# Ranking a planner's steps by the latest time they may begin, in an attention and two-layer kernel on one core

## The chip, the core and the metric

The kernel runs on one core of a Trainium2 chip. The metric is the device time of one execution in microseconds (us), smaller being better. A profile of one execution is at hand beside three timed runs.

The core has engines that run side by side, each with its own queue of instructions: TensorE (PE) multiplies matrices, and PEld is its loading of weights; VectorE (DVE) and ScalarE (ACT) do elementwise work and read the results from TensorE's accumulation banks; GpSimd (POOL) does a little elementwise work; SyncE (SP) here only issues DMAs. An instruction that waits for another engine holds up what stands behind it in its own queue.

## The reference

For 4 batches, 12 heads, 448 positions and 64 columns a head, in float32:

```python
scores = q @ k.T / sqrt(64) - log(448)
x = sigmoid(scores) @ v              # laid out as 1792 tokens x 768
h = x @ w_in                         # 768 x 2048
x = (h * cos(h)) @ w_out             # 2048 x 768
g, val = x @ w_gate, x @ w_val       # 768 x 1536 each
out = (g * sigmoid(g) * val) @ w_out2  # 1536 x 768
```

## The kernel before

**Numbers in two parts.** A float32 operand is split into a high part that TensorE takes at full speed (a copy to that type, mostly on ACT) and a low part (the operand minus the high part, always on DVE). A product is then three matmuls: high x high, high x low, low x high. The first needs only the high parts, so TensorE can begin a product whose low part is still missing, and then stops after one or two matmuls.

**Attention** (lines 511 to 625) comes first, in an order written out by hand. Its result X1 is kept as high and low parts in two large tiles, x0 and x1, one for each half of the tokens.

**The first layer** is 8 chunks of 256 columns of w_in by 4 groups of 448 tokens. For each such unit TensorE does two *ups* (18 matmuls each, line 863), then h*cos(h) is made of each result (`h_cos_h`, line 639, and `split_g`), and three *downs* of 12 matmuls (line 720) multiply it by w_out. DVE adds each pair of down results into R (`accumulate`, line 674), which frees the two banks for a later down.

**The second layer** has its tokens in two halves h of 896, and 6 chunks each, so 12 units. A unit multiplies by w_gate (u = 0) and by w_val (u = 1), each as a 2x2 block product in seven products, numbered 1 to 7, where sums of blocks of X and of the weights stand in for the eighth (`seven`, line 741). They run in the order 1, 5, 2, 6, 7, 3, 4 with downs of the unit before them in between (`TWO`). The seven X operands of a half are made from R by `inputs` (line 480), a step per operand: for 5, 6, 7 and 4 a difference of blocks (DVE), then the high part (`to_hi`, line 488: ACT or DVE, whichever the planner expects to end first), then the low part (DVE). Operands 1, 5, 2, 6 lie in x0 and 7, 3, 4 in x1, over the operands that were there: those of the first layer, later those of the half before. The rest of x1 lends room to weight operands.

Weights arrive by DMA in tiles `t`; `operands` (line 383) splits them in pairs (products 1 and 2; 6 and 3; 7 and 4) and singly (5), and makes the sums of weight blocks in four steps (`combine`, line 386) on DVE or POOL. The line 236 is the helper through which nearly all DVE sums and differences go, 233 that of most ACT instructions, so a tile's name tells more than its line.

**Conversions** (line 299). Of weights that come in 64 bits a word the kernel makes float32 tiles first: a load to `raw`, six steps on ACT and DVE (lines 309 to 324, the last a sum on `cv` that the rows call ISA or CUSTOM), a store to scratch memory, from where `loads` fetches them as `t`. They go on from the attention until the end of the first half of the second layer. When they end, `raw` is lent to `loads` and to others.

**What sets the order.** Nothing of this is ordered by hand after the attention: all steps are tasks of a small planner (class `Order`). Its `run` repeats one choice. Of all tasks whose inputs it reckons to be there it takes the one with the least

```python
key = (start, task.rank)
```

where `start` is the reckoned time at which engine and input are both free. So the rank decides among steps that are ready when an engine comes free. Before, a rank goes by the kind of task and is given at `spawn`: 0 for TensorE's own sequence and the copies between its banks, 1 and 2 for other banks' work (`accumulate` 2), 2.5 to 3 for the activations and `h_cos_h` with its `split_g`, 3 for loads, 3.5 for `inputs`, 4 for weight operands, 6 for conversions. The planner only writes the instructions down in this order, engine by engine; on the chip each engine runs its list in order and waits on semaphores.

Of the kernel before, what the change touches and what calls it, by code (L numbers as in the profile page):

```python
# [73 lines left out]
class Order:  # L74
# [4 lines left out]

    def __init__(self):  # L80
        self.busy, self.ready, self.open, self.now = {}, [], 0, 0.0
# [14 lines left out]
    def advance(self, task, sent=None):  # L96
        now = self.now
        while True:
# [51 lines left out]
def block_kernel(  # L150
# [104 lines left out]


# [22 lines left out]
    for need in needs():  # L279
        for w, f, i, _ in need:  # L280
            if w.dtype == U64 and (w, f + i) not in todo:
                todo.append((w, f + i))
    todo = iter(todo)
# [15 lines left out]
    def conversions(raw=None, t=None, back=None):  # L299

        while not (back and ended):
# [3 lines left out]
            if not back:  # L305
                raw = yield raws
            yield move(raw.rearrange("p n two -> p (n two)"), flat(w[f]).bitcast(I32))
            yield LANDING
            yield act(0.95, out=raw[:, :, 0], in_=raw[:, :, 0].bitcast(U32), func=AF.Copy, scale=2.0 ** -29)
# [3 lines left out]
            yield absolute(t, raw[:, :, 1])  # L313
            yield {"DVE": 0.6}, lambda _: nc.vector.tensor_scalar(
                t, t, HI_MOST, HI_LEAST, op0=ALU.min, op1=ALU.max
            )
            yield {"DVE": 0.6}, lambda _: nc.vector.tensor_scalar(
                ti, ti, 3, 0x3FFFFFF8, op0=ALU.logical_shift_left, op1=ALU.bitwise_and
            )
# [3 lines left out]
            )  # L323
            yield vec(1.0, ti, ti, raw[:, :, 0], ADD)
# [58 lines left out]
    def operands():  # L383


        def combine(out, a, b, op):
# [3 lines left out]
            return {"DVE": 0.6, "POOL": 1.3}, do  # L390
# [9 lines left out]
        def lower(keys, s, t, lo, hi, size, room, free, done):  # L400
            yield vec(0.1 + size / 780, lo, t, f32(hi), SUB)
# [9 lines left out]
        def split(keys, t, free=None):  # L411
# [4 lines left out]
            yield copy(0.15 + size / 980, hi, t)  # L416
# [21 lines left out]
        for n in range(n_first, n_units):  # L438
            for u in range(2):
# [6 lines left out]
                yield combine(sums, a21, a22, ADD)  # L446
                yield combine(a21, a11, a21, SUB)
# [32 lines left out]
    def inputs(h):  # L480
# [158 lines left out]
    def h_cos_h(key, h, read):  # L639
# [3 lines left out]
        yield act(0.55, out=u, in_=h, func=AF.Copy, scale=INV2PI, bias=0.25)  # L643
        yield act(0.6, out=f, in_=u, func=AF.Copy, bias=MAGIC)
        yield {"DVE": 0.65}, lambda _: nc.vector.scalar_tensor_tensor(  # L645
            out=f, in0=f, scalar=MAGIC, in1=u, op0=ALU.subtract, op1=ALU.subtract
        )
        yield act(0.6, out=u, in_=f, func=AF.Sin, scale=-TWO_PI)
        yield vec(0.65, f, u, h, ALU.mult)
# [3 lines left out]
    def silu(z, h, read, done):  # L653
        yield act(0.6, out=z, in_=h, func=AF.Silu)
# [3 lines left out]
    def silu_val(key, z, z_done, h, read, free):  # L658
        yield z_done
        yield vec(0.65, z, z, h, ALU.mult)  # L660
# [13 lines left out]
    def accumulate(n, j, d, first):  # L674
# [3 lines left out]
        two, acc = banks[:, first:first + 2, :N], R[h][:, j, d:d + 2]  # L678
        if c == 0:
# [3 lines left out]
            yield copy(1.05, acc, two)  # L683
        else:
            yield vec(1.1, acc, two, acc, ADD)
# [50 lines left out]
    PRODUCT = 0.2025  # L736

    TWO = "15d26d73d4"
    LAST = ("1526d734", "15d26d73d4dd")

    def seven(n, u, turn, z, downs):
# [7 lines left out]
        def first_copy():  # L749
            got["b"] = yield b  # L750
            yield copy(0.55, got["b"], got["a"])
            copied.set()

        def second_copy():
            got["e"] = yield e
            yield copy(0.55, got["e"], got["a"])
            apart.set()

        def fifth():
            yield copy(0.55, keep["12"], got["d"])  # L760
            d.give(got["d"])

        def sum22():
            yield vec(0.65, keep["22"], keep["12"], got["a"], ADD)
# [3 lines left out]
        def sum12():  # L768
            yield vec(0.65, keep["12"], keep["12"], got["e"], ADD)
# [3 lines left out]
        def after(ij, h, read):  # L773
            key = (n, int(ij[0]) - 1, int(ij[1]) - 1)
            if not val:
# [4 lines left out]
                order.spawn(silu(z[ij][0], h, read, z[ij][1]), 2.5)  # L780
            else:
                if ij in ("22", "12"):
                    read = shared_keep
                order.spawn(silu_val(key, z[ij][0], z[ij][1], h, read, z[ij][2]), 3)

        for token in LAST[u] if n == n_units - 1 else TWO:
# [183 lines left out]
```

## Time and profile before

| | us |
|---|---|
| median of 3 timed runs | 1148.28 |
| lowest and highest of them | 1145.71, 1149.85 |
| profiled execution, its own time | 1157.76 |
| its span, first to last instruction | 1155.9 |
| PE busy in it | 1122.1 |
| DVE busy | 807.5 |
| ACT busy | 573.1 |
| POOL busy | 80.1 |

The profiled execution is 9.48 us above the median. The page's slices show PE full but for the attention at the start (the first four slices), two places, at about 620 to 680 us and at 870 to 900 us, and the end. The rows that matter stand below under their own heading.

### The profile page before, as it was taken

The page shows a single profiled execution, that of the slowest core. Times are in us where ns is not written, and L with a number is a line of the kernel's source. Part 1 is how long each engine was busy: PE and PEld are TensorE (multiplying, and loading weights), DVE is VectorE, ACT ScalarE, POOL GpSimd, SP SyncE. Part 2 cuts the span into 40 slices and gives each one's busy share as a digit, 9 for nine tenths or more (in the row PEclk, how much of TensorE's full clock was granted, in tenths as well). Part 3 has the DMA queues.
Part 4 walks back from the last instruction along what each step waited for, and adds up shares of the span by engine and source line. Part 5 has one row for each costly group of instructions (what it writes and reads, how often), then busy time and mean ns, then how long its engine had stood idle before and what let it go on. Part 6 is the DMA issues. An engine that isn't in the chain of part 4 may idle for free.

```text
span 1155.9 us, 14399 instructions
## 1 busy us (share of the span) xinstructions
PE 1122.1 (97%) x5531; PEld 964.1 (83%) x5531; DVE 807.5 (70%) x1143; ACT 573.1 (50%) x858; POOL 80.1 (7%) x69
## 2 busy tenths in 40 slices
PE   9999999999999999999999799999997999999998
PEld 4555569999999999999998589999996999999996
DVE  6777745677777777777768967787888555556654
ACT  6877765645454544444444556443434344333330
POOL 0000000000000000000001110112203011102100
PEclk9999999999999999999999799999998999999999
DMA  9999723524343434334341334524321421121102
GB/s 251 286 277 264 206 109 125 166 98 145 110 150 110 150 110 142 118 123 138 109 137 41 109 124 148 181 88 157 138 84 59 143 83 55 55 69 55 49 8 96
DMA packets 51909, 146.43 MB, mean 127 GB/s; under 512 B 5760, under 2 KB 21120, under 8 KB 51840
## 3 DMA queue, kind: packets, MB, share of 16 engines
q1 hardware_dynamic: 51696, 145.28, 39.6%
q8 instruction: 43, 0.70, 0.2%
q10 hardware_dynamic: 144, 0.23, 0.1%
q14 instruction: 26, 0.21, 0.1%
HBM read 113.25 MB, written 32.24 MB: 126 GB/s over the span
## 4 chain that ended last, share of the span: by engine, by line
PE 89%; DVE 5%; DMA 4%; ACT 1%; issue 1%; SPq 0%; ACTq 0%; DVEq 0%
PE banks L720 35%; PE banks L809 27%; PE banks L863 21%; DMA raw<-in_qk 3%; PE banks L583 3%; PE banks L559 2%; PE banks L586 1%; DVE x L236 1%; DVE r L236 1%; DMA vs<-in_v 1%; DMA r<-in_w_out 1%; PE banks L571 1%; ACT a L549 0%; DVE r L320 0%; DVE x L530 0%
## 5 line engine op out<-in xcount | busy, mean ns | idle before, releaser
L720 PE MATMUL banks<-g,wb 128*128 128x448 f32 x1080 | 244.5, 368 | 1.2 <-DVE g L236 1.1
L236 DVE TENSOR_TENSOR r<-banks,r 128x896 f32<-128x896 f32 x144 | 156.9, 1090 | 117.8 <-PE banks L720 116.6
L720 PEld LDWEIGHTS banks<-g,wb 128*128 128x128 f32 x1080 | 202.8, 188 | 21.3 <-DVE g L236 1.4
L720 PE MATMUL banks<-g,wa 128*128 128x448 f32 x792 | 181.6, 368 | 1.7 <-DVE g L236 1.4
L720 PEld LDWEIGHTS banks<-g,wa 128*128 128x128 f32 x792 | 148.5, 188 | 16.7 <-DVE g L236 1.8
L809 PE MATMUL banks<-x,wb 128*128 128x448 f32 x666 | 149.5, 373 | 8.2 <-DVE x L236 5.4
L809 PEld LDWEIGHTS banks<-x,wb 128*128 128x128 f32 x666 | 127.0, 191 | 21.3 <-DVE x L236 6.5
L863 PE MATMUL banks<-x,wb 128*128 128x448 f32 x648 | 139.7, 368 | 0.0
L863 PEld LDWEIGHTS banks<-x,wb 128*128 128x128 f32 x648 | 121.6, 188 | 12.3
L233 ACT ACTIVATE g<-u 128x448 fp32r<-128x448 f32 x106 | 61.2, 578 | 142.5 <-DVE u L236 130.3
L233 ACT ACTIVATE u<-banks 128x448 f32<-128x448 f32 x106 | 57.4, 541 | 134.6 <-PE banks L863 79.5
L233 ACT ACTIVATE u<-u 128x448 f32<-128x448 f32 x148 | 85.3, 576 | 65.6 <-DVE u L645 34.8
L863 PE MATMUL banks<-x,wa 128*128 128x448 f32 x504 | 108.5, 369 | 0.0
L236 DVE TENSOR_TENSOR u<-u,banks 128x448 f32<-128x448 f32 x126 | 77.4, 614 | 41.5 <-PE banks L809 34.2
L863 PEld LDWEIGHTS banks<-x,wa 128*128 128x128 f32 x504 | 94.6, 188 | 9.9 <-issue 0.4
L809 PE MATMUL banks<-x,wa 128*128 128x448 f32 x432 | 94.7, 366 | 0.7 <-ACT banks L233 0.7
L809 PEld LDWEIGHTS banks<-x,wa 128*128 128x128 f32 x432 | 81.0, 188 | 8.0 <-ACT banks L233 1.1
L809 PE MATMUL banks<-x,x 128*128 128x448 f32 x315 | 73.4, 382 | 8.7 <-DVE x L236 8.6
L236 DVE TENSOR_TENSOR g<-u,g 128x448 fp32r<-128x448 f32 x106 | 68.6, 650 | 15.0 <-ACT g L233 14.9
L645 DVE SCALAR_TENSOR_TENSOR u<-u 128x448 f32<-128x448 f32 x64 | 39.9, 624 | 52.0 <-ACT u L233 51.5
L809 PEld LDWEIGHTS banks<-x,x 128*128 128x128 f32 x315 | 61.9, 198 | 15.6 <-DVE x L236 9.0
L549 ACT ACTIVATE a<-banks,r 128x896 f32<-128x896 f32 x72 | 67.2, 1003 | 7.2 <-PE banks L559 7.1
(88 smaller groups left out, 1274.2 us busy)
## 6 DMA issues: line engine op xcount, KB each, us to landing
raw<-in_w_out SPq DMA_DIRECT2D x22, 768.0 KB, 4.6
raw<-in_qk SPq DMA_DIRECT2D x47, 224.0 KB, 8.6
raw<-in_w_gate SPq DMA_DIRECT2D x12, 768.0 KB, 4.5
raw<-in_w_val SPq DMA_DIRECT2D x12, 768.0 KB, 4.7
vs<-in_v SPq DMA_DIRECT2D x24, 320.0 KB, 6.9
t<-swv SPq DMA_DIRECT2D x20, 384.0 KB, 3.1
t<-swg SPq DMA_DIRECT2D x19, 384.0 KB, 3.9
t<-swd SPq DMA_DIRECT2D x34, 192.0 KB, 2.5
```

What stands on the lines that cost most here:

```text
L233: return {"ACT": time}, lambda _: nc.scalar.activation(**kw)
L236: return {"DVE": time}, lambda _: nc.vector.tensor_tensor(out=out, in0=in0, in1=in1, op=op)
L549: nc.scalar.activation(out=a, in_=sc, func=AF.Sigmoid, bias=nlog, scale=1.0 / math.sqrt(D))
L559: nc.tensor.matmul(sc[:, j], lhsT=k[half, m, c * P:(c + 1) * P], rhs=q[half, p], start=n == 0, stop=n == 2,)
L571: nc.tensor.matmul(sc, lhsT=kb[:, m], rhs=q[:, p], start=n == 0, stop=n == 2)
L583: nc.tensor.matmul(o[half], lhsT=vw[:, 2 * c + j], rhs=a[:, j], start=c == 0, stop=False)
L586: nc.tensor.matmul(o, lhsT=block[:, 1], rhs=prob.pop((i, NCH)), start=False, stop=True)
L645: yield {"DVE": 0.65}, lambda _: nc.vector.scalar_tensor_tensor(out=f, in0=f, scalar=MAGIC, in1=u, op0=ALU.subtract, op1=ALU.subtract)
L720: nc.tensor.matmul(banks[:, first + e - d, :N], lhsT=w[:, m, e % KH if layer == 2 else e, :], rhs=g[:, p], start=(i, m, p) == (0, 0, 0), s ...
L809: nc.tensor.matmul(bank, lhsT=w[:, m, k, :], rhs=x[:, k, p, :], start=(k, m, p) == (0, 0, 0) and i in (1, 5), stop=(k, m) == (KH - 1, 1), ...
L863: nc.tensor.matmul(out, lhsT=w[:, m, k, :], rhs=x[:, k, p, cols], start=(k, m, p) == (0, 0, 0), stop=(k, m) == (KD - 1, 1),)
```

## The change

Every step beside TensorE now gets a rank of its own: the latest time at which it may begin if TensorE is never to wait for it. A table `due` is made beforehand from TensorE's sequence alone: the start of each up, product and down when all matmuls follow each other without a gap at 0.2025 us. A step's rank is the start of what waits for it less an allowance for the steps that come in between. The planner takes the rank from the step (`advance`) and is otherwise as it was: `start` still comes first in the key. TensorE's own sequence is the same. A down's `accumulate` is ranked by the down after the next; an X operand's steps by the product in which it is first used; a conversion by the first use of its weights less 25 us. Tasks that only issue DMAs for loads keep rank 3.

```diff
@@ Order.advance
-                task.wants, task.do = want
+                task.wants, task.do, task.rank = want if len(want) > 2 else (*want, task.rank)
@@ block_kernel, after units
+    time = 0.0
+    for key, products in steps():
+        due[key] = time
+        time += products * PRODUCT
+    end = time
...
+    def by(time, step):
+        return (*step, time)
@@ conversions
+                uses.setdefault((id(w), 2 * c + i), due[key] - 25.0)
...
-            yield absolute(t, raw[:, :, 1])
+            yield by(time, absolute(t, raw[:, :, 1]))
@@ operands
-            yield vec(0.1 + size / 780, lo, t, f32(hi), SUB)
+            yield by(due[keys[0]] - 1.2, vec(0.1 + size / 780, lo, t, f32(hi), SUB))
...
-                yield combine(a11, sums, a11, SUB)
-                yield combine(a12, a12, a11, SUB)
+                yield combine(a11, sums, a11, SUB, due[n, u, 6] - 4.0)
+                yield combine(a12, a12, a11, SUB, due[n, u, 3] - 4.0)
@@ inputs
+            time = due[n_first + h * (NF2 // 2), 0, i]
             if parts:
-                yield vec(1.6, t, parts[0], parts[1], SUB)
+                yield by(time - 5.0, vec(1.6, t, parts[0], parts[1], SUB))
             hi, lo = X[i][:, :, 0], X[i][:, :, 1]
-            yield to_hi(hi, t)
-            yield vec(1.6, lo, t, f32(hi), SUB)
+            yield by(time - 3.2, to_hi(hi, t))
+            yield by(time - 1.7, vec(1.6, lo, t, f32(hi), SUB))
@@ split_g (the like in h_cos_h, silu, silu_val, and the copies and sums of seven)
+        time = due["down", n, j, 0]
-        yield copy(0.6, g[:, 0], f)
-        yield vec(0.65, g[:, 1], f, f32(g[:, 0]), SUB)
+        yield by(time - 1.5, copy(0.6, g[:, 0], f))
+        yield by(time - 0.8, vec(0.65, g[:, 1], f, f32(g[:, 0]), SUB))
@@ accumulate
+        time = after_down(n, j if layer == 2 else 0, d) - 1.3
+        if layer == 1 and c == NF1 // 2 - 1:
+            time = min(time, due[n_first + h * (NF2 // 2), 0, 1] - 6.0)
-            yield vec(1.1, acc, two, acc, ADD)
+            yield by(time, vec(1.1, acc, two, acc, ADD))
```

TensorE's instructions stand in the same order as before, and no engine's order differs within the attention. The rows below are those of DVE at two places. In them r0 and r1 are the two halves of R, x0 and x1 hold the X operands and, at their rest, weights; `x<-r` is a low part (or, as CAST, a high part) of an X operand, `r<-r` the difference of blocks before it, `r<-banks` an accumulate, `wb<-t`, `wa<-raw` and `x1<-raw0` low parts of weights, and `g` an operand of the downs.

DVE where the first layer ends and the second begins, before:

```order
L314 TENSOR_SCALAR cv_1480<-cv_1480 128x768
L236 TENSOR_TENSOR g2_1486<-u2_1490,g2_1486 128x448
L493 CAST x0_66<-r0_64 128x3x448
L645 SCALAR_TENSOR_TENSOR u0_1488<-u0_1488 128x448
L236 TENSOR_TENSOR r1_65<-banks_63,r1_65 128x896
L236 TENSOR_TENSOR u0_1488<-u0_1488,banks_63 128x448
L236 TENSOR_TENSOR x0_66<-r0_64,x0_66 128x3x448
L236 TENSOR_TENSOR r1_65<-banks_63,r1_65 128x896
L236 TENSOR_TENSOR g3_1487<-u0_1488,g3_1487 128x448
L236 TENSOR_TENSOR wb0_1481<-t_68,wb0_1481 128x768
L236 TENSOR_TENSOR x0_66<-r0_64,x0_66 128x3x448
L236 TENSOR_TENSOR x1_67<-sum_1479,x1_67 128x384
```

and now:

```order
L395 TENSOR_SCALAR cv_1480<-cv_1480 128x768
L237 TENSOR_TENSOR x0_66<-r0_64,x0_66 128x3x448
L237 TENSOR_TENSOR g2_1486<-u2_1490,g2_1486 128x448
L237 TENSOR_TENSOR r1_65<-banks_63,r1_65 128x896
L727 SCALAR_TENSOR_TENSOR u0_1488<-u0_1488 128x448
L237 TENSOR_TENSOR wb0_1481<-t_68,wb0_1481 128x768
L237 TENSOR_TENSOR u0_1488<-u0_1488,banks_63 128x448
L237 TENSOR_TENSOR r1_65<-banks_63,r1_65 128x896
L237 TENSOR_TENSOR g3_1487<-u0_1488,g3_1487 128x448
L237 TENSOR_TENSOR x1_67<-sum_1479,x1_67 128x384
L237 TENSOR_TENSOR x0_66<-r0_64,x0_66 128x3x448
L237 TENSOR_TENSOR wb1_1482<-t_68,wb1_1482 128x768
```

The CAST, a high part of operand 5, has left DVE's list, as has that of operand 4 further down: all seven high parts stand on ACT now. The low part of operand 5 and the weights wb0 stand earlier, and the first step on the last chain for the downs (line 645, now 727) stands behind an accumulate.

DVE where the first half of the second layer ends and the second half begins, before:

```order
L236 TENSOR_TENSOR r0_64<-banks_63,r0_64 128x896
L236 TENSOR_TENSOR u2_1490<-u2_1490,u1_1489 128x448
L236 TENSOR_TENSOR g3_1487<-u2_1490,g3_1487 128x448
L236 TENSOR_TENSOR u0_1488<-u0_1488,banks_63 128x448
L236 TENSOR_TENSOR g2_1486<-u2_1490,g2_1486 128x448
L236 TENSOR_TENSOR x0_66<-r1_65,x0_66 128x3x448
L236 TENSOR_TENSOR g1_1485<-u0_1488,g1_1485 128x448
L236 TENSOR_TENSOR r1_65<-r1_65 128x1344
L236 TENSOR_TENSOR wb2_1483<-t_68,wb2_1483 128x768
L236 TENSOR_TENSOR wa0_69<-raw0_1477,wa0_69 128x768
L236 TENSOR_TENSOR x1_67<-r1_65,x1_67 128x3x448
L236 TENSOR_TENSOR x1_67<-raw0_1477,x1_67 128x768
```

and now:

```order
L237 TENSOR_TENSOR wb2_1483<-t_68,wb2_1483 128x768
L237 TENSOR_TENSOR r1_65<-r1_65 128x1344
L237 TENSOR_TENSOR x1_67<-raw0_1477,x1_67 128x768
L237 TENSOR_TENSOR u0_1488<-u0_1488,banks_63 128x448
L237 TENSOR_TENSOR r0_64<-banks_63,r0_64 128x896
L237 TENSOR_TENSOR u2_1490<-u2_1490,banks_63 128x448
L237 TENSOR_TENSOR x1_67<-sum_1479,x1_67 128x384
L237 TENSOR_TENSOR x0_66<-r1_65,x0_66 128x3x448
L237 TENSOR_TENSOR g1_1485<-u2_1490,g1_1485 128x448
L237 TENSOR_TENSOR r1_65<-r1_65 128x1344
```

The weights of products 1 and 2 of the new half, `x1<-raw0`, stood last of these and stand third now, ahead of the accumulate, the low part of operand 6 and the difference for operand 7. Two of the values `g2` and `g3` have gone behind what is shown.

## Rows read from the trace of the kernel before

**Rows 1.** The page's head and its line of TensorE: busy us, share, instructions.

```profile
span 1155.9 us, 14399 instructions
PE 1122.1 (97%) x5531; PEld 964.1 (83%) x5531; DVE 807.5 (70%) x1143; ACT 573.1 (50%) x858; POOL 80.1 (7%) x69
```

**Rows 2.** Whom PE waited for: total us, times, longest.

```profile
PE banks L809 <- DVE x L236: 14.0, 4, 8.6
...
PE banks L720 <- DVE g L236: 2.5, 2, 1.4
PE banks L809 <- DVE x L493: 2.2, 1, 2.2
```

**Rows 3.** Stretches: us; PE, PEld, DVE, ACT, POOL busy; clock; DMA share; GB/s.

```profile
160.00:622.00 462.00, 462.00 (x2237) 419.56 (x2237) 336.01 (x462) 235.28 (x373) 2.04 (x2) 1.00 0.38 129
622.00:672.00 50.00, 39.62 (x166) 33.47 (x164) 44.35 (x45) 23.66 (x33) 9.79 (x6) 0.86 0.30 95
672.00:876.00 204.00, 203.83 (x1006) 188.89 (x1007) 156.18 (x207) 99.46 (x152) 33.34 (x29) 1.00 0.38 126
876.00:896.00 20.00, 11.37 (x43) 10.03 (x42) 17.07 (x18) 8.71 (x13) 6.32 (x3) 0.74 0.17 50
```

**Rows 4.** PE in order of time between the layers: start, us, instruction, idle before.

```profile
645.78 0.47 PE L809 MATMUL banks<-x,wb 128*128 128x448 f32 x1 [0.62 <-ACT banks L233]
646.82 2.10 PE L809 MATMUL banks<-x,wb 128*128 128x448 f32 x9 [0.57 <-DVE x L236]
652.12 3.36 PE L809 MATMUL banks<-x,wb 128*128 128x448 f32 x8 [3.20 <-DVE x L236]
657.65 0.74 PE L809 MATMUL banks<-x,wb 128*128 128x448 f32 x1 [2.17 <-DVE x L493]
659.98 3.36 PE L809 MATMUL banks<-x,wb 128*128 128x448 f32 x8 [1.59 <-DVE x L236]
```

**Rows 5.** DVE in order of time, same place.

```profile
623.67 1.54 DVE L493 CAST x<-r 128x1344 fp32r<-128x1344 f32 x1
...
648.02 1.77 DVE L236 CUSTOM_DVE_ANT_0 cv<-raw,cv 128x1536 uint16<-128x1536 uint16 x1
...
656.05 1.54 DVE L493 CAST x<-r 128x1344 fp32r<-128x1344 f32 x1
...
658.38 1.55 DVE L236 TENSOR_TENSOR x<-r,x 128x1344 fp32r<-128x1344 f32 x1
...
661.58 0.55 DVE L314 TENSOR_SCALAR cv<-cv 128x768 f32<-128x768 f32 x1
...
663.76 0.96 DVE L236 CUSTOM_DVE_ANT_0 cv<-raw,cv 128x1536 uint16<-128x1536 uint16 x1
```

**Rows 6.** PE in order of time between the halves of the second layer.

```profile
878.39 0.57 PE L809 MATMUL banks<-x,x 128*128 128x448 f32 x2
887.59 6.32 PE L809 MATMUL banks<-x,x 128*128 128x448 f32 x16 [8.63 <-DVE x L236]
```

**Rows 7.** DVE in order of time, same place.

```profile
856.70 1.09 DVE L236 TENSOR_TENSOR r<-banks,r 128x896 f32<-128x896 f32 x1
...
876.76 1.09 DVE L236 TENSOR_TENSOR r<-banks,r 128x896 f32<-128x896 f32 x1 [1.04 <-PE banks L720]
...
885.12 1.55 DVE L236 TENSOR_TENSOR x<-r,x 128x1344 fp32r<-128x1344 f32 x1
886.59 0.95 DVE L236 TENSOR_TENSOR x<-raw,x 128x768 fp32r<-128x768 f32 x1
```

**Rows 8.** POOL in order of time, same place: a combine of weight blocks.

```profile
888.62 3.66 POOL L389 TENSOR_TENSOR raw<-raw 128x384 f32<-128x384 f32 x1 [16.08 <-DVE raw L389]
892.23 1.00 POOL L389 TENSOR_TENSOR sum<-t 128x384 f32<-128x384 f32 x1
```

**Rows 9.** Line 320 alone, one instruction a conversion: us, DVE busy (count), clock, DMA.

```profile
672.00:860.00 188.00, 12.41 (x13) 1.00 0.38 125
```

**Rows 10.** DVE at the end of the program.

```profile
1135.90 1.15 DVE L236 TENSOR_TENSOR g<-u,g 128x448 fp32r<-128x448 f32 x2
```

More of the change, by code (lines that the diff above doesn't have):

```diff
@@ L253, in block_kernel, with between, tokens, steps @@
     n_units = len(units)
+    PRODUCT = 0.2025
+    TWO = "15d26d73d4"
+    LAST = ("1526d734", "15d26d73d4dd")
+    due, down_steps, sevens = {}, [], []
+    def between(n):
+        return ((1, 2) if n > 1 else (0, 3))
+    def tokens(n, u):
+        return LAST[u] if n == n_units - 1 else TWO
+    def steps():
+        left = []
+        def some(k):
+            for key in left[:k]:
+                down_steps.append(key)
+                yield key, 12
+            del left[:k]
+        for n, (layer, _, c) in enumerate(units):
+            if layer == 1:
+                for i in range(2):
+                    yield (n, i), 18
+                    yield from some(between(n)[i])
+            else:
+                if n == n_first:
+                    yield from some(len(left))
+                for u in range(2):
+                    sevens.append((n, u))
+                    for token in tokens(n, u):
+                        if token == "d":
+                            yield from some(1)
+                        else:
+                            yield (n, u, int(token)), 9
+            left.extend(("down", n, j, d) for j in range(layer) for d in range(0, KD, 2))
+        yield from some(len(left))
+    time = 0.0
[3 more added lines that the diff above has]
+    end = time
+    for n, (layer, g, c) in enumerate(units):
+        for i in range(2):
+            if layer == 1:
+                due.setdefault(("u", c, i), due[n, i])
+                due.setdefault(("d", c, i), due["down", n, 0, 0])
+            else:
+                for k in range(2):
+                    due["d", n, i, k] = due["down", n, 0, 2 * k]
+    def by(time, step):
+        return (*step, time)
+    def after_seven(n, u, i):
+        at = sevens.index((n, u)) + 1
+        return due[(*sevens[at], i)] if at < len(sevens) else end
+    def after_down(n, j, d):
+        at = down_steps.index(("down", n, j, d)) + 2
+        return due[down_steps[at]] if at < len(down_steps) else end
     names = {id(w): nm for w, nm in zip((w_in, w_out, w_gate, w_val, w_out2), ("wi", "wo", "wg", "wv", "wd"))}
@@ L383, in operands, with combine @@
     def operands():
-        def combine(out, a, b, op):
+        def combine(out, a, b, op, time):
             def do(engine):
@@ L389, in do @@
                 on.tensor_tensor(out=out, in0=a, in1=b, op=op)
-            return {"DVE": 0.6, "POOL": 1.3}, do
+            return {"DVE": 0.6, "POOL": 1.3}, do, time
         def take():
@@ L750, in first_copy @@
             got["b"] = yield b
[L751 removed]
+            yield by(due[n, u, 2] - 0.6, copy(0.55, got["b"], got["a"]))
             copied.set()
@@ L774, in after @@
             key = (n, int(ij[0]) - 1, int(ij[1]) - 1)
+            time = {"11": after_seven(n, u, 7) - 1.5, "21": after_seven(n, u, 5) - 0.8}.get(ij, end)
             if not val:
@@ L779, in after @@
                     z[ij] = (z["two"][:, int(ij == "21")], order.event(), z["leave"])
-                order.spawn(silu(z[ij][0], h, read, z[ij][1]), 2.5)
+                order.spawn(silu(z[ij][0], h, read, z[ij][1], min(time, due["down", n, 0, 0] - 6.0)), 0)
             else:
@@ L783, in after @@
                     read = shared_keep
-                order.spawn(silu_val(key, z[ij][0], z[ij][1], h, read, z[ij][2]), 3)
-        for token in LAST[u] if n == n_units - 1 else TWO:
+                order.spawn(silu_val(key, z[ij][0], z[ij][1], h, read, z[ij][2], time), 0)
+        for token in tokens(n, u):
             if token == "d":
@@ L881, in tensor_engine @@
                     yield from up(n, i, upbanks[next(turn) % 4])
-                    for _ in range(((1, 2) if n > 1 else (0, 3))[i]):
+                    for _ in range(between(n)[i]):
                         yield from some(downs)
@@ L902, in block_kernel @@
             returned.append(order.event())
-            order.spawn(conversions(raw, t, returned[-1]), 6)
+            order.spawn(conversions(raw, t, returned[-1]), end)
         attention()
@@ L907, in block_kernel @@
                 raws.give(mp.tile([P, WT, 2], I32, tag=f"raw{i}", name=f"raw{i}"))
-                order.spawn(conversions(), 6)
+                order.spawn(conversions(), end)
             sum_room.append(mp.tile([P, W], F32, tag="sum", name="sum"))
```

60 lines of the change are left out of this document (34 added, 26 removed).

## The prediction

> **What bounds the kernel now.** I read the head of the page first: PE is busy for 97% of the span [rows 1]. A faster DVE or ACT can therefore only help where PE stands still or runs slowly. The table of stretches says where that is [rows 3]. From 160 to 622 us and from 672 to 876 us PE has no gap worth naming (203.83 of 204.00 us in the second), and in the second of them a matmul takes 204.00 / 1006 = 0.203 us. Two short stretches are different. From 622 to 672 us, where the first layer ends, PE did 166 matmuls, which at 0.203 us are 33.7 us of 50: 16.3 us are lost. From 876 to 896 us, where the halves of the second layer meet, it did 43, or 8.7 us of 20: 11.3 us are lost. In both the granted clock fell, to means of 0.86 and 0.74 of full speed. Third I read whom PE waited for [rows 2]: low parts and high parts of X operands and weights (`x`, lines 236 and 493) for 16.2 us, and operands of the downs (`g`) for 2.5 us. All come from DVE, which is busy for 44.35 of the 50 us and 17.07 of the 20 [rows 3]. ACT is busy for less than half of either. So in these places DVE's list sets the end, and its order and what stands in it matter; elsewhere neither does.
>
> **Place one, between the layers.** PE's last long stop is in product 4 of the first unit: its first matmul starts at 657.65 us when the high part of operand 4 is there, and the other eight at 659.98 us, after the low part [rows 4]. That low part starts on DVE at 658.38 us, behind a CAST at 656.05 us [rows 5].
>
> What the change does to DVE's list ahead of that low part: two CASTs go to ACT, 2 x 1.54 = 3.1 us less; one step of a conversion of 0.55 us goes ahead of the stretch; the low part of a further weight tile comes in, 0.95 us [rows 5, 7]. One combine moves to POOL and another comes from it. That is 3.1 + 0.5 - 0.9 = 2.7 us less work on a list that is nearly always busy. ACT has room for the two high parts.
>
> The other end: I laid the new list out with the trace's durations, each instruction as soon as its engine and inputs allow. The low parts of operands 6, 7 and 3 come in steps of about one difference, one weight and one low part, and the last low part ends near 654.3 us instead of 659.9: 5.6 us. This leaves out that DVE and POOL disturb each other, as the last step of a conversion shows, 1.77 us at 648.02 while POOL works and 0.96 at 663.76 [rows 5]. I take 4 us, between 2.7 and 5.6. One thing gets worse in this layout: line 645's step for the last chain of the downs stands behind an accumulate that waits for TensorE, some 1.5 us later than before. Earlier weights win this back, and the value g3 is there at about 630.4 us in both, so the downs before the new layer start neither earlier nor later.
>
> PE still has a stop of about 4 us ahead of operand 4's low part in this layout, so I leave the slow matmuls that follow (eight in 3.36 us, which at 0.203 are 1.6) in the time. If the clock holds they are a gain of their own: 2 x (3.36 - 1.62) = 3.5 us for the two groups of eight [rows 4].
>
> **Place two, between the halves.** PE begins product 1 of the new half at 878.39 us, does two matmuls and waits 8.63 us, until 887.59 [rows 6]. What it waits for is no X operand: it is the low part of that product's weights, `x<-raw`, which begins at 886.59 us [rows 7]. The ranks of before put it last, with kind 4. Behind the wait sixteen matmuls take 6.32 us, where 16 x 0.203 are 3.2 [rows 6]: 3.1 us for the clock. The whole is 8.6 + 3.1 = 11.7 us.
>
> In the new list these weights stand ahead of the accumulate that began at 876.76 us. Is DVE on time there? From the accumulate at 856.70 us to that one there are 20.1 us [rows 7]. The new list holds between them three accumulates (1.09 each), five X steps (1.55), four weight tiles (0.95), one step of a conversion (0.96) and four small ones (about 0.61): 3.3 + 7.8 + 3.8 + 1.0 + 2.4 = 18.3 us. It fits, with 1.8 us for waiting. Then product 1 runs without a stop, and the wait and the slow clock both go.
>
> What is late next? In the same layout product 5's weights are ready at 879.6 us and wanted at 880.2; operand 6 at 881.1 and wanted at 886.3; its weights, which now hang on two combines on POOL, at 884 and wanted at 886.3; the accumulate that frees the banks for the third down at 888.6, wanted at 894.2; and operand 4's low part at 895.4 and wanted at 896.6. So 11.7 us with 1.2 us to spare at the narrowest of the late points.
>
> Two combines in a row on POOL are what speaks against it: one took 3.66 us in this very stretch, another 1.00 us [rows 8]. With 3.66 for both, the weights of product 6 are there at 885.4 us, DVE's list behind them is late by 1.4 us, and operand 4 comes at 896.8 against 896.6. The nearest row is the long one. I take off 2.2 us for this and for DVE's own delays and say 9.5; the ends are 0 (another operand as late as the one that goes) and 11.7.
>
> The Trainium skill says of this, in SBUF — State Buffer, Who interferes with whom, that a VectorE instruction with both inputs in SBUF and a GpSimd instruction that reads SBUF shut each other out, and that whichever began first keeps the port for its whole length. The trace agrees as far as a POOL combine takes 1.00 to 3.66 us. By that rule DVE too would stop for each of the two combines, up to 2 x 1.0 us at POOL's undisturbed length, and place two would give 11.7 - 2.0 = 9.7 us.
>
> **The end, and what costs nothing.** Near the end PE waits for two `g` in a row, the second being the one it needs [rows 2, 10]. The new list has the needed one first: 1.15 / 2 = 0.6 us. In the layers' long stretches DVE is busy 336 of 462 and 156 of 204 us [rows 3]; another order there changes nothing as long as PE finds its operands, so it costs 0. That cover goes if a step that PE needs soon stands behind one that waits; bounds in the rivals. Seven conversions, as a net change, have one more step on DVE in place of ACT, 0.55 us each at the length of its neighbour [rows 5]; that is some 4 us of DVE time in hundreds. SP's loads and stores change places by a few entries, always with the tile that they free or fill.
>
> **Sum.** 4 + 9.5 + 0.6 = 14 us. The profiled execution of 1157.76 us would become 1143.7. The executions differ in the pace of all matmuls, not in these waits, so I take the same 14 us off the median: 1148.28 - 14 = 1134.3 us.
>
> **Rivals.**
>
> *More is won (0.16).* The clock holds in place one (3.5 us), the layout's 5.6 us come true, and place two gives 11.7: 3.5 + 5.6 + 11.7 + 0.6 = 21.4 us, 1127 us. For it: rows 6 show how dear a stop is beyond its length. Against: a stop of some 4 us is left in place one.
>
> *The wait moves on (0.18).* Place two wins only half, since what was put off (accumulates, `g` of the old half, differences) must be done within the next 20 us, and PE then stops at product 7 or 4: 2.7 + 5 + 0.6 = 8 us, 1140 us. For it: DVE has 17.07 busy us of 20 there [rows 3] and spare of only 1.2 us in the layout. Against: before, DVE reached the same steps with a list of the same length.
>
> *Nothing that counts changes (0.08).* A load that TensorE's operands hang on is no earlier, so the weights of product 1 come at the same time although they stand earlier; or the gain at one place is lost at the other. 1148 us. Against: the weights' tile is used in the new list only well behind other work on it; the trace names DVE and no DMA as the releaser [rows 6].
>
> *Slower (0.08).* One mechanism: conversions no longer come last. From 672 to 860 us there are 13 [rows 9], each about 3.1 us of DVE (four instructions, from 661.58 to 663.76 + 0.96 = 664.72 us) [rows 5], and a rank of 25 us before use puts one that is behind ahead of weights that PE wants next. If each makes PE wait, the gain is eaten from 14 / 13 = 1.1 us a conversion on; at 1.6 us it is 13 x 1.6 - 14 = 6.8 us, 1155 us. For it: these conversions run while DVE is three quarters busy. Against: PE's total loss there is 0.17 us [rows 3], and `start` still goes before the rank, so a conversion waits its turn.
>
> **Numbers.** The forecast, 1134 us, has 0.50; its own range is 1130 to 1139 us. A measurement here tells 0.3%, or 3.4 us, from no change. Faster by more than that (below 1144.8): 0.50 + 0.16 + 0.18 = 0.84; within it 0.08; slower 0.08. The range for 8 in 10 takes in both other faster cases and ends near the border of no change: 1125 to 1145 us.
>
> **What would show it.** Right: in place two, no stop of PE over 2 us, the clock there near 1, and product 1 not split after two matmuls; in place one the last low part of the first unit's operands some 4 us nearer to the end of the first layer, no high part of an X operand on DVE, and PE's wait for `x` down from 16.2 us to 6 or less; long stretches still without gaps. Wrong: a wait of PE of several us in 160 to 622 or 672 to 876, above all one that a weight tile ended with a conversion ahead of it; or in place two a stop for wb, wa or x a few products later that is as long as the old one.

## The result, and the profile after

| | kernel before | changed kernel | ratio, 95% interval |
|---|---|---|---|
| first timing, 6 runs each | 1146.99 us | 1136.44 us | 0.9893 [0.9855, 0.9930] |
| second, 23 and 6 runs | 1151.92 us | 1137.13 us | 0.9882 [0.9838, 0.9925] |
| third, 17 and 6 runs | 1154.33 us | 1135.74 us | 0.9853 [0.9803, 0.9902] |

The forecast was 1134 us, 14 us less than the kernel before. The profiled execution took 1141.06 us after 1157.76, its span 1139.3 after 1155.9. These 16.6 us are not all the change's: the pace of all matmuls wanders from run to run (last section), so below only stretches between the same two matmuls are compared.

Line numbers moved: 233 is now 234, 236 is 237, 491 is 569, 645 is 727, 720 is 805, 809 is 890, 863 is 944, 389 is 467.

First TensorE's waits of the changed kernel: total us, times, longest. They answer [rows 2].

```profile
PE banks L890 <- DVE x L237: 3.5, 3, 2.0
...
PE banks L890 <- ACT x L569: 1.5, 1, 1.5
```

The waits for `x`, 16.2 us before, are 3.5 + 1.5 = 5.0 us. The stretches, with the columns of [rows 3]:

```profile
160.00:622.00 462.00, 462.00 (x2237) 419.65 (x2236) 337.49 (x465) 224.75 (x358) 2.42 (x2) 1.00 0.36 124
622.00:672.00 50.00, 42.69 (x187) 36.94 (x187) 43.16 (x51) 28.43 (x40) 8.97 (x6) 0.93 0.30 95
672.00:876.00 204.00, 203.93 (x1007) 188.68 (x1005) 161.70 (x207) 104.62 (x156) 36.54 (x32) 1.00 0.42 140
876.00:896.00 20.00, 18.96 (x93) 17.12 (x92) 20.00 (x21) 11.73 (x17) 4.84 (x4) 1.00 0.33 105
```

The long stretches are without gaps, as before. Place two's granted clock is 1.00 (the 2.4 GHz level) instead of 0.74, place one's 0.93 instead of 0.86; a mean below 1.00 here mixes the two levels, 1.2 and 2.4 GHz.

Place one, TensorE in order of time (start, us, instruction, idle before), against [rows 4]:

```profile
621.40 5.74 PE L805 MATMUL banks<-g,wa 128*128 128x448 f32 x27
627.76 0.47 PE L805 MATMUL banks<-g,wa 128*128 128x448 f32 x1 [0.62 <-ACT g L234]
629.35 8.31 PE L805 MATMUL banks<-g,wa 128*128 128x448 f32 x32 [1.12 <-DVE g L237]
637.50 1.99 PE L890 MATMUL banks<-x,wb 128*128 128x448 f32 x9
...
648.69 1.89 PE L890 MATMUL banks<-x,wb 128*128 128x448 f32 x8 [0.53 <-DVE x L237]
652.05 0.47 PE L890 MATMUL banks<-x,wb 128*128 128x448 f32 x1 [1.47 <-ACT x L569]
654.50 3.19 PE L890 MATMUL banks<-x,wb 128*128 128x448 f32 x8 [1.97 <-DVE x L237]
657.53 5.74 PE L890 MATMUL banks<-x,x 128*128 128x448 f32 x27
...
665.82 5.74 PE L890 MATMUL banks<-x,wa 128*128 128x448 f32 x27 [0.69 <-ACT banks L234]
```

The same stretch of the kernel before, from the end of the last up to product 7 of the second seven; it and [rows 4] together give the sums below:

```profile
623.18 5.95 PE L720 MATMUL banks<-g,wa 128*128 128x448 f32 x28
630.54 4.32 PE L720 MATMUL banks<-g,wa 128*128 128x448 f32 x20 [1.41 <-DVE g L236]
635.17 2.70 PE L720 MATMUL banks<-g,wa 128*128 128x448 f32 x12 [0.31 <-DVE r L236]
637.71 1.99 PE L809 MATMUL banks<-x,wb 128*128 128x448 f32 x9
...
663.14 6.53 PE L809 MATMUL banks<-x,x 128*128 128x448 f32 x27
...
672.17 5.74 PE L809 MATMUL banks<-x,wa 128*128 128x448 f32 x27 [0.68 <-ACT banks L233]
```

That product 7 starts at 672.17 us before and at 665.82 now: 48.99 and 44.42 us from the end of the last up, so place one wins 4.57 us. The downs (up to product 1) went from 14.53 to 16.10 us, and the X part (product 1 to that product 7) from 34.46 to 28.32. These two are no loss and gain of their own, for TensorE's last long stop in the place, for operand 4's low part, lies behind both: a later start of product 1 shortens the waits on the way to that stop. Counted from the end of the last up, that stop ends at 36.80 us before (659.98 - 623.18) and at 33.10 now (654.50 - 621.40), 3.70 us sooner; the other 0.87 us come behind it (12.19 and 11.32 us up to product 7).

DVE in the same place has no CAST any more, and operand 4's low part, the row that answers to 658.38 us in [rows 5], is

```profile
652.89 1.55 DVE L237 TENSOR_TENSOR x<-r,x 128x1344 fp32r<-128x1344 f32 x1
```

31.49 us behind the end of the last up, where it was 35.20: 3.7 us nearer.

Place two, TensorE, against [rows 6] and two more rows of before, product 7 and product 5 of the next seven; then TensorE now, DVE, against [rows 7]; then POOL, against [rows 8]:

```profile
902.26 1.98 PE L809 MATMUL banks<-x,wb 128*128 128x448 f32 x9
...
911.99 1.99 PE L809 MATMUL banks<-x,x 128*128 128x448 f32 x9
```

```profile
872.35 3.81 PE L890 MATMUL banks<-x,x 128*128 128x448 f32 x18
...
884.51 1.98 PE L890 MATMUL banks<-x,wb 128*128 128x448 f32 x9
...
890.59 0.36 PE L890 MATMUL banks<-x,wb 128*128 128x448 f32 x1
892.00 3.78 PE L890 MATMUL banks<-x,wb 128*128 128x448 f32 x17 [1.04 <-DVE x L237]
895.61 2.02 PE L890 MATMUL banks<-x,x 128*128 128x448 f32 x9
```

```profile
870.19 0.95 DVE L237 TENSOR_TENSOR x<-raw,x 128x768 fp32r<-128x768 f32 x1
...
875.21 1.43 DVE L237 TENSOR_TENSOR g<-u,g 128x448 fp32r<-128x448 f32 x1
876.57 2.37 DVE L237 TENSOR_TENSOR r<-r 128x1344 f32<-128x1344 f32 x1
...
889.04 1.44 DVE L237 TENSOR_TENSOR u<-u,u 128x448 f32<-128x448 f32 x1
890.39 1.55 DVE L237 TENSOR_TENSOR x<-r,x 128x1344 fp32r<-128x1344 f32 x1
```

```profile
871.28 1.02 POOL L467 TENSOR_TENSOR raw<-sum,raw 128x384 f32<-128x384 f32 x1 [6.29 <-DVE x L237]
872.39 1.02 POOL L467 TENSOR_TENSOR raw<-raw 128x384 f32<-128x384 f32 x1
873.90 2.27 POOL L467 TENSOR_TENSOR sum<-t 128x384 f32<-128x384 f32 x1 [0.49 <-DVE x L237]
876.24 1.27 POOL L467 TENSOR_TENSOR t<-t 128x384 f32<-128x384 f32 x1
...
888.78 1.21 POOL L467 TENSOR_TENSOR t<-t 128x384 f32<-128x384 f32 x1
```

The low part of product 1's weights is through at 871.1 us, ahead of product 1 at 872.35, which runs in one piece. Product 1 to product 7 is 12.16 us; before it was 902.26 - 878.39 = 23.87. A new stop of 1.04 us stands at product 4, for operand 4's low part (890.39 us). To product 5 of the next seven it is 23.26 us after 33.60 (878.39 to 911.99): 10.3 us won.

At the end the `g` wait of 1.11 us (of the 2.5 in [rows 2]) is now one of 0.57. In sum 4.6 + 10.3 + 0.5 = 15.4 us; the three timings say 12 to 17.

### The profile page after: what moved, and what is told of

The parts are those of the page before. It is cut to its first block, busy times and chain, and to the rows that moved or that the text cites. A ratio compares the mean times of both kernels' runs of the same rounds, so it can differ in the third digit from the quotient of the medians.

```text
span 1139.3 us, 14408 instructions
## 1 busy us (share of the span) xinstructions
PE 1117.3 (98%) x5531; PEld 959.8 (84%) x5531; DVE 806.3 (71%) x1145; ACT 572.0 (50%) x855; POOL 78.8 (7%) x70
## 4 chain that ended last, share of the span: by engine, by line
PE 90%; DVE 5%; ACT 2%; issue 1%; DMA 1%; ACTq 0%; DVEq 0%
PE banks L805 35%; PE banks L890 25%; PE banks L944 21%; PE banks L662 4%; PE banks L638 3%; PE banks L665 1%; DVE x L237 1%; DVE r L237 1%; ACT a L628 1%; PE banks L650 1%; DMA vs<-in_v 1%; DVE r L398 1%; DVE x L609 0%; DMA raw<-in_qk 0%; ACT r L369 0%
## 5 line engine op out<-in xcount | busy, mean ns | idle before, releaser
L237 DVE TENSOR_TENSOR u<-u,banks 128x448 f32<-128x448 f32 x130 | 80.0, 615 | 41.0 <-PE banks L890 33.9
L234 ACT ACTIVATE wb<-t 128x768 fp32r<-128x768 f32 x58 | 48.3, 840 | 46.7 <-PE banks L944 18.0
L237 DVE TENSOR_TENSOR wb<-t,wb 128x768 fp32r<-128x768 f32 x58 | 56.2, 975 | 20.2 <-ACT wb L234 19.8
```

The lines of the kernel that those rows point to most:

```text
L234: return {"ACT": time}, lambda _: nc.scalar.activation(**kw)
L237: return {"DVE": time}, lambda _: nc.vector.tensor_tensor(out=out, in0=in0, in1=in1, op=op)
```

## The experiments

Times are medians; every ratio is to the kernel before, timed beside it. "Place one" is the stretch from the end of the last up to product 7 of the second seven, "place two" from product 1 to product 7 of the second half (to product 5 of the next seven in brackets), both from each kernel's own trace; where product 1 itself starts late it is counted from where it would have followed the matmuls before it without a gap.

| kernel | us | ratio, 95% interval | place one | place two |
|---|---|---|---|---|
| before | | | 48.99 | 23.87 (33.60) |
| changed, first trace | 1136.44 | 0.9893 [0.9855, 0.9930] | 44.42 | 12.16 (23.26) |
| changed, second | 1137.13 | 0.9882 [0.9838, 0.9925] | 44.43 | 12.16 (23.01) |
| changed, third | 1135.74 | 0.9853 [0.9803, 0.9902] | 46.08 | 12.16 (23.03) |
| one step last | 1148.00 | 0.9963 [0.9938, 0.9987] | 45.57 | 23.68 (33.40) |
| conversions last | 1151.12 | 1.0011 [0.9983, 1.0039] | 44.40 | 27.28 (37.20) |
| conversions 80 us ahead | 1136.53 | 0.9899 [0.9861, 0.9936] | 44.99 | 12.60 (26.76) |
| high parts on DVE | 1149.70 | 1.0011 [0.9973, 1.0050] | 51.04 | 17.53 (33.12) |
| before, high parts on ACT | 1145.43 | 0.9967 [0.9937, 0.9997] | 48.11 | 19.63 (29.55) |
| before, weights first | 1169.11 | 1.0164 [1.0112, 1.0216] | 49.62 | 17.32 (34.18) |
| before, wait filled | 1150.76 | 1.0001 [0.9967, 1.0036] | 49.35 | 21.28 (31.20) |
| X due 4 us sooner | 1134.82 | 0.9862 [0.9817, 0.9907] | 40.92 | 13.08 (22.96) |
| the same again | 1134.83 | 0.9849 [0.9810, 0.9888] | 42.43 | 12.88 (22.74) |

### The changed kernel, one step ranked last

```diff
-            yield by(due[keys[0]] - 1.2, vec(0.1 + size / 780, lo, t, f32(hi), SUB))
+            time = end if keys[0] == (n_first + NF2 // 2, 0, 1) else due[keys[0]] - 1.2
+            yield by(time, vec(0.1 + size / 780, lo, t, f32(hi), SUB))
```

> The changed kernel with one single instruction put back: the low part of product 1's weights at the start of the second half is ranked after all else, as its kind stood behind all else before. It is ready as early as in the changed kernel. Theory, its place in DVE's list alone makes place two: in this kernel's list it stands behind operand 7's low part, some 12 us later than the 870.19 us of the changed kernel, so TensorE stops some 9 to 11 us at product 1, the sixteen matmuls behind it take 6 us again, and operand 4's stop of 1 us goes; 10 to 13 us slower than the changed kernel, ratio to before 0.996 to 1.000. Rival, the weights came earlier because their tile did and not for the rank: then DVE finds a gap for it and the time stays within 3 us of the changed kernel.

TensorE, then that step on DVE and on ACT its high part:

```profile
867.43 0.57 PE L891 MATMUL banks<-x,x 128*128 128x448 f32 x2
877.60 5.16 PE L891 MATMUL banks<-x,x 128*128 128x448 f32 x16 [9.59 <-DVE x L237]
```

```profile
876.59 0.95 DVE L237 TENSOR_TENSOR x<-raw,x 128x768 fp32r<-128x768 f32 x1
```

```profile
860.28 0.83 ACT L234 ACTIVATE x<-raw 128x768 fp32r<-128x768 f32 x1
```

The high part is done at 861.1 us, so the tile was there; DVE comes to the low part 15.5 us later. The stop is back at 9.59 us, operand 4's is gone, place two is 23.68 us, and the kernel is some 12 us slower than the changed one beside it (1135.74, third timing). The place of one instruction in DVE's list takes back the whole of place two.

### The changed kernel, conversions last

```diff
-            time = uses[id(w), f]
+            time = end
```

> The changed kernel, but every step of a conversion ranked after all else (its due time is the end of the program). Rival of the prediction, conversions 25 us ahead of use disturb weights that TensorE wants next: then this is faster than the changed kernel, by up to 1 us a conversion. My theory: the conversions cost nothing, and their lead is what brings the new half's weights in time. In this kernel's list the last conversion moves past 850 us and the low part of product 1's weights behind the X operands again, so place two gets a stop of 6 to 10 us at product 1 with the slow clock behind it; place one and its 4.6 us stay as in the changed kernel. Sum 8 to 12 us slower than the changed kernel: ratio to before 0.996 to 1.000. No gaps in 160 to 622 and 672 to 860 us in either.

```profile
879.74 1.11 PE L890 MATMUL banks<-x,x 128*128 128x448 f32 x2 [11.14 <-ACT x L234]
882.27 4.92 PE L890 MATMUL banks<-x,x 128*128 128x448 f32 x16 [1.42 <-DVE x L237]
```

Longer than expected, and the high part is missing too, so it is another mechanism than the one above. DVE, then SP's queue in order of time, then whom SP waited for (total us, times, longest) show it:

```profile
849.42 0.95 DVE L398 SCALAR_TENSOR_TENSOR cv<-raw,cv 128x768 int32<-128x768 int32 x1
...
863.09 0.95 DVE L237 CUSTOM_DVE_ANT_0 cv<-raw,cv 128x1536 uint16<-128x1536 uint16 x1
```

```profile
845.32 0.32 SPq L243 DMA_DIRECT2D t<-swd  x1
864.07 0.32 SPq L243 DMA_DIRECT2D swd<-cv  x1
```

```profile
SPq L243 <- DVE cv L237: 374.6, 54, 18.4
```

The last step of the last conversion waits 13 us for its turn on DVE, its store (`swd<-cv`) waits for it at the head of SP's queue, and behind the store stand all the loads of the next tiles. SP does nothing from 845.6 to 864.07 us, its longest wait for `cv` (18.4 us); in the changed kernel the same store goes at 852.65. The load of the new half's weights (`raw<-swg`) goes at 867.98 instead of 856.28, and lands 4.7 us later, at about 872.7. ACT comes to its high part only at 878.86, behind the high parts of two X operands in its list (874.29 and 876.91), and DVE to the low part at 881.27. The kernel is 14 us slower than the changed one; how much of that is the late load and how much its later place in the two lists is not separated.

### The changed kernel, conversions 80 us ahead

```diff
-                uses.setdefault((id(w), 2 * c + i), due[key] - 25.0)
+                uses.setdefault((id(w), 2 * c + i), due[key] - 80.0)
```

> The changed kernel with the conversions due 80 us ahead of their tile's first use in place of 25. The slower rival of the prediction says that a conversion ahead of a weight tile makes TensorE wait, 1 us or more each: with them further ahead, some 20 conversions up to 860 us would show stops of that kind in 160 to 622 and 672 to 860 us, 10 us or more slower than the changed kernel. Theory, they cost nothing in the long stretches because DVE is three quarters busy and weights are a tile ahead: no gap there, the product 1 stop stays away, and the time is within 4 us of the changed kernel (ratio to before 0.987 to 0.992).

The theory holds: no wait stands on line 944, the ups of the first layer, TensorE is busy for 194.00 of 194.00 us from 672 to 866, product 1 does not stop, and the time is the changed kernel's within the noise. Operand 4 is later in place two (stops of 0.81 and 1.39 us), which with the matmuls behind it costs some 3.5 us. The prediction's slower rival has no support even at this lead.

### The changed kernel, all high parts on DVE

```diff
-            return {"ACT": 1.55, "DVE": 1.2}, do
+            return {"DVE": 1.2}, do
```

> The changed kernel with the high part of every X operand on DVE only (it was mostly ACT): five more CASTs of 1.55 us on DVE around each of the two places. In place one the stretch of X operands, product 1 to the first weight group after product 3, took 34.46 us before, 28.32 in the changed kernel and 28.31 in the kernel before with all high parts on ACT. Theory, it is DVE's load and not the ranks that made those 6.1 us: here 33 to 38 us, as before or longer; the downs ahead of it win 1.5 to 3 us because g's high part no longer stands behind a CAST on ACT; place two gets back a stop of 3 to 6 us at product 1 or at operands 6, 7 and 4. Sum 8 to 15 us slower than the changed kernel, ratio to before 0.996 to 1.002. Rival, the order alone made the gain: under 3 us slower than the changed kernel.

The figures came: X part 37.19 us (625.68 to 662.87), downs 13.85 us, in place two stops at products 1, 7, 3 and 4, about 13 us slower than the changed kernel by the medians. Operand 4's stop ends 38.32 us behind the last up (650.15 - 611.83), later than the 36.80 of the kernel before. With due times and all high parts on DVE the gain is nil. What the ranks would give with two CASTs on DVE, as before, was not run.

### The kernel before, all high parts on ACT

```diff
-            return {"ACT": 1.55, "DVE": 1.2}, do
+            return {"ACT": 1.55}, do
```

> The kernel before with its kind ranks; the high parts of all X operands on ACT only, so that the four CASTs on DVE (two in place one, two in place two, 1.54 to 1.55 us each) leave DVE's list. Theory, DVE's list is the bound in both places: place one gains the two CASTs, some 3 us (operand 4's low part 3 us nearer to the end of the first layer); in place two the low part of product 1's weights is still behind the pile of g and X steps, but nearer by three or four entries, so the 8.6 us stop shrinks to some 4 to 6 us and does not go; in sum 5 to 8 us faster than before, ratio about 0.994. Rival, the ranks alone matter and DVE's work is no bound: under 1.5 us, ratio 1.000 to 0.999.

```profile
630.10 0.47 PE L720 MATMUL banks<-g,wa 128*128 128x448 f32 x1 [3.10 <-ACT g L233]
631.96 9.26 PE L720 MATMUL banks<-g,wa 128*128 128x448 f32 x32 [1.40 <-DVE g L236]
641.06 2.02 PE L809 MATMUL banks<-x,wb 128*128 128x448 f32 x9
...
658.00 3.36 PE L809 MATMUL banks<-x,wb 128*128 128x448 f32 x8 [1.91 <-DVE x L236]
...
669.37 2.90 PE L809 MATMUL banks<-x,wa 128*128 128x448 f32 x13 [0.71 <-ACT banks L233]
...
880.40 6.29 PE L809 MATMUL banks<-x,x 128*128 128x448 f32 x16 [4.25 <-DVE x L236]
```

The X part is 669.37 - 641.06 = 28.31 us, as short as in the changed kernel, but only because it starts later: the downs take 19.80 us after 14.53, for late `g`. Counted from the end of the last up (621.26), operand 4's stop ends at 36.74 us, where it was 36.80, and place one as a whole wins 0.9 us, behind that stop. So the 3 us expected there did not come. In part that is DVE now standing idle, for 0.77, 0.24 and 0.87 us at 623, 635 and 638 us, until down results come. Place two's stop shrank to 4.25 us, as expected, and place two wins 4.1 us to the next seven. The ratio says 4 us.

### The kernel before, weights ahead by kind

```diff
-        order.spawn(operands(), 4)
+        order.spawn(operands(), 2.4)
```

and the same number for `lower`.

> The kernel before, still with ranks by kind, but the weights' steps ranked 2.4 in place of 4, ahead of the X operands and of g's last steps. Rival to my account, it is enough that the weights no longer stand last: then the 8.63 us stop at product 1 goes and all of place two's 11 us is won, about 1137 us beside 1147 to 1152 of before. Theory, DVE's list is full there and what counts is which step is due, so another fixed order only chooses another victim: the stop at product 1 goes, but operands 6, 7 and 4 stand six to twelve entries later in DVE's list (operand 6's low part some 3 us, 7's and 4's up to 10 us), place one loses 3 to 8 us and place two wins 5 us at most; from 4 us faster to 8 us slower than before, with the new stops ended by X operands.

Worse than my worst figure, 19 us slower. Product 1 ran without a stop, but X operands stopped products 6, 7, 3 and 4 (0.62, 1.79, 0.37 and 2.86 us); place two is 34.18 us to the next seven, after 33.60. What I had not foreseen is a third victim, the steps on `u` that read the products out of TensorE's banks, five times from product 5 of this seven on:

```profile
PE banks L809 <- DVE u L236: 11.1, 5, 2.5
```

So this other fixed order does not do it.

### The kernel before, the wait filled

```diff
+            if (n, u, i) == (n_first + NF2 // 2, 0, 1):
+                yield x_ready[h, i]
+
+                def fill(_, bank=got["a"]):
+                    x = X[1]
+                    for r in range(36):
+                        nc.tensor.matmul(bank, lhsT=x[:, 0, 0, :P], rhs=x[:, 0, 0, :], start=True, stop=True)
+
+                yield {"PE": 36 * PRODUCT}, fill
```

> The kernel before with 36 more matmuls of the same size ahead of product 1 of the second half, into that product's own bank, from an operand that is already there; product 1 then writes over them, so the output holds nothing of them. They take 36 x 0.203 = 7.3 us of the 8.6 us in which TensorE stood still. Theory, the sixteen matmuls behind the stop took 6.32 us in place of 3.2 because TensorE had stood still: now they take 3.2 to 3.6, and the kernel is up to 3 us faster although it does more work; product 1's wait for its weights is 1 to 2 us. Rival, they were slow for another reason (their operands, other engines at SBUF): still 6 us, and the time within 0.5 us of before. The order elsewhere on DVE moves a little with it; place one should stay at 34 to 35 us.

```profile
869.04 7.46 PE L807 MATMUL banks<-x 128*128 128x448 f32 x36
...
878.24 3.57 PE L818 MATMUL banks<-x,x 128*128 128x448 f32 x16 [1.34 <-DVE x L236]
```

The sixteen matmuls take 3.57 us instead of 6.32 [rows 6], and place two is 2.6 us shorter with 36 matmuls more in it: the stop itself made them slow. The granted clock says the same: 0.52 from 887 to 894 us before, near the 1.2 GHz level, after a stop of 8.63 us; 1.00 from 867 to 882 us here, where TensorE was busy for 13.66 of the 15 us. The timing cannot show it (interval of 8 us).

### A better version, and the changed kernel beside it

```diff
-            time = due[n_first + h * (NF2 // 2), 0, i]
+            time = due[n_first + h * (NF2 // 2), 0, i] - 4.0
```

> The changed kernel with the due times of the X operands' three steps 4 us earlier. It is the try at a better version: after the change PE still waits some 7 us in place one, last for operand 4's low part, and 1.04 us at product 4 in place two. Theory, the order among X steps and accumulates still matters there: operand 4's low part comes 2 to 3.4 us earlier in both places, 2 to 4 us faster than the changed kernel (ratio to before 0.986). Rival, what is put off (accumulates, weights) is late instead: within 1 us of the changed kernel or slower.

> The changed kernel once more, beside the others on the same chip. The trace's account is 15.8 us (4.6 in place one, 10.7 in place two, 0.5 at the end); the first timing said 12.3 us with an interval of 8 to 17. Theory, the account is the whole: ratio 0.986 to 0.988 (14 to 16 us). Rival, part of it is eaten by a slower pace of all matmuls or by chance in the profiled executions: ratio 0.990 to 0.993 (8 to 11 us).

> The changed kernel with the X operands' due times 4 us earlier, a second time, beside the changed kernel on the same chip. The first trace says 3.5 us in place one (40.92 us from the last up to the weights after product 3, 44.42 and 44.43 in the changed kernel) and nothing in place two. Theory: 3 to 4 us faster than the changed kernel here too, some 0.3%, which the medians may just show. Rival: the downs or a later g give it back, medians within 1 us.

> The changed kernel a third time, as the other side of that comparison: 0.987 to 0.990 of before, 44.4 us in place one and 12.2 us from product 1 to product 7 in place two, and whole stretches in which a matmul takes 202.7 or 206.7 ns, other ones than in the two traces so far.

The traces agree with the theory in place one (40.92 and 42.43 us against 44.42, 44.43 and 46.08) and operand 4's stop in place two is gone, with 0.6 and 0.3 us for a `g` in its stead. The medians are 2.3 and 0.9 us lower; the means of all runs are 1133.8 (12) and 1135.5 us (18), single runs lie from 1124 to 1142. That it beats the changed kernel is shown by stretches, not by times.

## Why the prediction held, point by point

**Place two, 9.5 us; measured 10.3.** The mechanism is shown: put one step back and it is all lost. The 8.63 us and the slow sixteen went whole (23.87 - 12.16 = 11.71 us, the 11.7 of the working), and the filled wait shows that the clock's share hung on the stop. What was taken off for the next late operand, 2.2 us, measured 1.4. The layout's "1.2 us to spare" at operand 4 was not there. Its low part was put 895.4 - 878.39 = 17.0 us behind product 1 and ends 891.94 - 872.35 = 19.6 behind it. Three steps on DVE that ran beside POOL make 2.5 of the 2.6: 1.43 and 1.44 us where 0.62 and 0.61 are usual, 2.37 where 1.55 is. POOL's two combines in a row, which I had feared at 3.66 us, took 1.02 each. So the delay came from the side that I had put second.

The Trainium skill, SBUF — State Buffer, Who interferes with whom, has a VectorE instruction with both inputs in SBUF and a GpSimd one that reads SBUF keep each other out. The trace agrees: each of the three ends when the GpSimd step beside it has ended and its own usual length has passed, to 0.15 us. The GpSimd steps end at 876.17, 877.51 and 889.99 us, so the ends would be 876.79, 879.06 and 890.60; they are 876.64, 878.94 and 890.48. Beside the two combines of 1.02 us DVE mostly ran steps that read one input from a bank (`u<-u,banks`, `r<-banks,r`), and these kept their lengths (0.61, 1.08 and 0.60 us). So the 9.7 us that the prediction worked out by that rule came near the measured 10.3 through other GpSimd steps than the two that it counted.

**Place one, 4 us; measured 4.6, 4.6 and 2.9 in the three traces.** The mechanism held, and its size too: operand 4's stop ends 3.70 us nearer to the last up (3.67 and 3.53 in the other two traces), between the two ends of the working and near the 4 taken. The rest is the pace behind that stop, which the sum had left out: 27 matmuls take 5.74 us where 6.53 stood before, but 7.10 in the third trace. So how close the 4 came to the 4.6 of the first trace is in part luck.

One step of the prediction failed: "so the downs before the new layer start neither earlier nor later". The late step was seen, the stops behind it were not: 0.62 and 1.12 us, and 32 matmuls in 8.31 us where 4.32 + 2.70 stood before; product 1 starts 1.57 us later. By the end of the place nothing of this is left to see, because the last stop lies behind it. For the same reason the 6.14 us by which the X part is shorter are not the gain: they are 3.70 + 0.87 + 1.57. The group of eight that now runs in 1.89 us for 3.36 lies ahead of that stop too; the group behind it took 3.19 of 3.36, so the 3.5 us that the rival "more is won" counts for the two groups did not come.

The CASTs' move to ACT alone is shown not to be enough: with kind ranks the stop ended at 36.74 us, no sooner than before. The CASTs back on DVE, with due ranks, lose it all (38.32). So the gain here is shown for both together; what the ranks give without the CASTs' move stays open.

**The end, 0.6 us; measured 0.5.**

**The conversions.** "It costs 0" is right for the long stretches, and the slower rival fell with the 80 us lead. But I weighed their due times only as a risk. They are a part of the gain: without them the loads stand behind a store that waits for DVE, the new half's weights come late in ACT's and DVE's lists, and the kernel is no faster than before. I had asked of SP's queue only whether entries change places, not what a store at its head holds up.

**The rival "the wait moves on"** happened in the changed kernel at 1 us, and in full where weights went first by kind (place two 34.18 us after 33.60).

**What the time says.** 15.4 us by the trace and 14 forecast; the first timing said 10.5 by its medians, the others 14.8 and 18.6. Between the first two traces of the changed kernel the spread is the matmuls' pace (last section) and not the waits; that this holds for all the timed runs is not shown.

## What to carry to other kernels

Look for the one step on which TensorE's longest stop ends, and ask whether it was ready long before its turn: if so, its place in one engine's list can be the whole price, as it was in place two, and the slow matmuls behind the stop go with it. Rank by due time rather than move one kind forward: the one other fixed order tried here found other victims. Give due times also to work that feeds a queue, since a late store at its head holds up every load behind it. And measure a stretch from a point ahead of it that the change does not move to one behind its last stop: the two CASTs alone seemed to win 6 us in the X part, and won 0.9 in place one, because the X part had only started later.

## What the runs showed of the hardware that was not expected

A matmul of 448 columns has two paces with the granted clock at 1.00 in both: a group of 18 starts 3.65 or 3.72 us before the next, 202.7 or 206.7 ns each. The changed kernel ran product 1 and 5 of the second half at the first and went on at the second from the stop at product 4 (895.61) to the last stop (1120.69 us): 225.08 us. In its second trace the same stretch, from 896.24 to 1117.00 us, kept the first pace and took 220.76. That is 4.3 us, more than the 3.7 by which the two spans differ. Which pace holds changes at stops and also without one, in either kernel, and the clock of the page does not tell them apart. What sets it stays open; by an estimate from the two paces (4 ns each) it alone can move a run of some 4600 such matmuls by up to 18 us.
